# An adaLN block on one core: where norm 1's scale and shift are applied, the split of row transpositions, and the order at the entry of mixing

## The chip, the cores and the metric

The kernel runs on one core of a Trainium2 chip. Its time is the device time in microseconds; the median of the kernel before over three runs is 1981.68 us (1977.05 to 1985.39). The engines are TensorE (PE, with its weight loads shown apart as PEld), VectorE (DVE), ScalarE (ACT), GpSimd (POOL) and SyncE (SP), which issues most transfers. PE writes its results to PSUM, which has eight banks; each PSUM tile here takes one.

## The reference

One sequence of S = 2048 rows, D = 576 columns, F = 4608, 32 heads of 18 columns, a causal window of 256. `w_mod` makes six vectors from a condition vector `c`; the first two shift and scale the first layer norm.

```python
mod = (_silu(c) @ w_mod).reshape(c.shape[0], 6, 1, -1)
sa, ca, ga, sb, cb, gb = (mod[:, 0], mod[:, 1], mod[:, 2], mod[:, 3], mod[:, 4], mod[:, 5])
h = _layernorm(x) * (1 + ca) + sa
x = x + ga * _A_ref(h, A_wqkv, A_wo)      # attention: qkv, softmax over 256 keys, @ wo
h = _layernorm(x) * (1 + cb) + sb
x = x + gb * _B_ref(h, B_w1, B_w2, B_w3, B_w4)

# _B_ref(x, w1, w2, w3, w4)
h = _gelu(_layernorm(x) @ w1)             # mixing: the four quarters of h's columns
hs = shifted(h) @ w2                      # are shifted by +1, -1, +2, -2 rows
x1 = x + hs
return x1 + _gelu(_layernorm(x1) @ w3) @ w4   # channel MLP
```

All inputs and the output are f32.

## The kernel before

**Products.** Each large matmul is made of three products of a high and a low part of both operands (fp32r), over four chunks of 128 of D and a tail of 64: 14 instructions per output tile (`products`). So every weight and every activation is split: a copy to fp32r gives the high part, a subtraction the low part. A chunk of the tail holds high and low part above each other in one 128-row chunk.

**Order.** The program is a list of events (time, function) that `play` runs in the order of their times. In the attention phase PE's instructions keep this order, while the other engines' are placed by the framework's scheduler, as PE's are in the later phases. The unit of time in attention is one attention unit: 4 heads and 512 queries, 32 of them (4 query groups, `g`, by 8). Times below zero are the prologue. A function that asks for a tile of a tag waits, on the chip, until an earlier tile of that tag is free: the number of buffers of each tag (`self.pb` for PSUM) therefore sets who waits for whom.

**Prologue.** `cond` computes SiLU of `c`. `mod_col` (L218) computes one vector of the modulation with 25 narrow products per vector (one column each), all in f32: the scale `ca` first, the shift `sa` later. The scale goes into the weights: `w_split` multiplies each chunk of Wqkv by `ca` (ACT for the high part, DVE for the low part, L242, five of each per chunk), `v_split` does so for the V weights (L270). The shift becomes a bias: `w_bias` (L250, per chunk of 128 columns of Q and K) and `v_bias` (L281), added when the projections are evicted.

**Rows to columns.** `x_norm` normalizes a block of 128 rows (on DVE, L108, or ACT, L106), `x_tr` transposes it with `split9`: the main part (L69, four transpositions into one bank, then the ACT copy L70 and the DVE subtraction L71) and the tail (L73, then L74 and L75). In the prologue main and tail have two banks, afterwards both take the one bank of tag "tr". The result `hT` holds 512 rows.

**Attention.** Projections of Q and K (L311, 14 instructions, one bank of tag "mm") are evicted by ACT (L333) and DVE (L334) into the tile `qe` and go to DRAM; those of V are evicted by DVE (L364). From DRAM Q and K come back per unit. Scores (L393) go through banks of tag "sc" to a masked maximum on DVE (L394), 16 score tiles per unit; their transposed counterpart X (L427) goes through "st" to the exponential on ACT (L440); `av` (L451) and its transposition (L463, into the tile of tag "oT") end a unit, and the rows go to DRAM. The PSUM banks are:

```python
self.pb = {"sc": 3, "st": 2, "av": 1, "mm": 1, "tr": 1}
```

The projections of group g+1 and the modulation's vectors 2 to 5 (`modvec`, POOL, L483) are spread between the units of group g.

**Output projection.** `s4(t)` reads 128 attention rows (`or` or `s4rows`) from DRAM, transposes them with `split9` into the single tile of tag "oT", multiplies by Wo (L616), adds the residual, normalizes twice and writes rows `xn` for mixing. Row blocks 0 to 11 run beside the last units of attention; blocks 12 to 15 at the start of mixing, with event times from -0.7 on, while the times of mixing itself count from 0.

**Mixing and MLP.** `stage1` loads normalized rows and transposes them (`xnT`), `stage2` multiplies by w1 (L771) and applies the GELU and the shifts, `stage3` multiplies by w2 (L822), normalizes and transposes again (`LT`). The channel MLP goes over 18 groups of 256 of F: up (L896), GELU (L902), down (L921), accumulation (L925); its weights are loaded and split by `weights(fg)` (L88 and L89), for the first group at the start of the phase.

Of the kernel before, what the change touches and what calls it, by code (L numbers as in the profile page):

```python
# [9 lines left out]
F32 = mybir.dt.float32  # L10
# [8 lines left out]
D = 576  # L19
F = 4608  # L20
P = 128
# [30 lines left out]
class Kern:  # L52
# [12 lines left out]
    def split9(self, row, L, cs, name, tags=("tr", "tr")):  # L65
        nc = self.nc
        pa = self.ps.tile([P, KC, P], F32, tag=tags[0], name=name + "pa", bufs=self.pb[tags[0]])
        for k in range(KC):
            nc.tensor.transpose(pa[:, k, :], row[:, k * P:(k + 1) * P], self.ident)  # L69
        nc.scalar.copy(L[:, 0:KC, cs], pa)  # L70
        nc.vector.tensor_tensor(out=L[:, KC:2 * KC, cs], in0=pa, in1=L[:, 0:KC, cs].bitcast(F32), op=ALU.subtract)  # L71
        pb = self.ps.tile([TAIL, P], F32, tag=tags[1], name=name + "pb", bufs=self.pb[tags[1]])
        nc.tensor.transpose(pb, row[:, KC * P:D], self.ident)  # L73
        nc.scalar.copy(L[:TAIL, 2 * KC, cs], pb)  # L74
        nc.vector.tensor_tensor(out=L[TAIL:, 2 * KC, cs], in0=pb, in1=L[:TAIL, 2 * KC, cs].bitcast(F32), op=ALU.subtract)  # L75
# [37 lines left out]
    def setup(self, stack):  # L113
# [11 lines left out]
        self.identb = self.cst.tile([P, P], BF16, name="identb")  # L125
        nc.vector.tensor_copy(self.identb, self.ident)
# [9 lines left out]
    def phase_a(self):  # L136
# [9 lines left out]
        self.pb = {"sc": 3, "st": 2, "av": 1, "mm": 1, "tr": 1}  # L146
        with ExitStack() as st:
# [7 lines left out]
            maskb = kp.tile([P, 2, P], BF16, name="maskb")  # L155
            silu = kp.tile([P, KC + 1], F32, name="silu")
            sa = kp.tile([P, KC + 1], F32, name="sa")
            ca = kp.tile([P, KC + 1], F32, name="ca")
            bqk = kp.tile([P, 9], F32, name="bqk")
            bv = kp.tile([P, D], F32, name="bv")  # L160
            ones = kp.tile([P, 1], F32, name="ones")
            pw = None

            def consts():
                nc.gpsimd.memset(ones, 1.0)
                for i in range(3):
                    nc.gpsimd.memset(Q[i].bitcast(F32), 0.0)
                    nc.gpsimd.memset(K[i][96:128].bitcast(F32), 1.0)
                    if i == 0:
                        nc.gpsimd.memset(mask, 0.0)  # L170
                        nc.gpsimd.affine_select(out=mask[:, 0:P], in_=mask[:, 0:P], pattern=[[1, P]], compare_op=ALU.is_gt, fill=NEG, base=0, channel_multiplier=-1)
                        nc.gpsimd.affine_select(out=mask[:, 2 * P:], in_=mask[:, 2 * P:], pattern=[[-1, P]], compare_op=ALU.is_ge, fill=NEG, base=0, channel_multiplier=1)
                        nc.gpsimd.memset(maskb, 0.0)
                        nc.gpsimd.affine_select(out=maskb[:, 1, :], in_=maskb[:, 1, :], pattern=[[1, P]], compare_op=ALU.is_ge, fill=NEG, base=0, channel_multiplier=-1)
                        nc.gpsimd.affine_select(out=maskb[:, 0, :], in_=maskb[:, 0, :], pattern=[[-1, P]], compare_op=ALU.is_gt, fill=NEG, base=0, channel_multiplier=1)
                        for v in V[:4]:
                            nc.gpsimd.memset(v, 1.0)
                for v in V[4:]:
                    nc.gpsimd.memset(v, 1.0)
# [3 lines left out]
            def cond():  # L183
                ct = sm.tile([P, KC + 1], F32, name="ct", bufs=1)
                nc.vector.memset(ct, 0.0)
                with nc.allow_non_contiguous_dma("condition vector to partitions"):
                    nc.sync.dma_start(ct[:, 0:KC], self.c[0, 0:KC * P].rearrange("(k p) -> p k", p=P))
                    nc.sync.dma_start(ct[:TAIL, KC:KC + 1], self.c[0, KC * P:].rearrange("(k p) -> p k", p=TAIL))
# [788 lines left out]
```

## Time and profile before

| | |
|---|---|
| median of three runs | 1981.68 us (1977.05 to 1985.39) |
| profiled execution, own time | 1975.25 us |
| its span | 1973.5 us |
| PE busy | 1819.9 us, 92% |
| DVE busy | 961.7 us, 49% |
| ACT busy | 634.0 us, 32% |
| POOL busy | 384.4 us, 19% |
| HBM read, written | 107.81 MB, 50.73 MB |

The stages by their spans: the first score starts at 104.27 us; projections are interleaved with attention until about 629; then the output projection takes their place until 852.8; mixing begins and ends between there and about 1041; the channel MLP runs from 1070 to the end. A profile row of a group gives its line, engine, operation, output and inputs with their shape, the count, and behind the bar the busy time, the mean time of one in ns, and the idle time of the engine just before them with what ended most of it. A timeline row gives the start, the length and in brackets how long the engine had been idle and what released it. Rows of waits give, for a line, whom its engine stood idle for, the idle time in us and how often.

### The profile page before, as it was taken

What the parts mean: (1) busy time and instruction counts of PE and PEld (TensorE: products, weight loads), DVE (VectorE), ACT (ScalarE), POOL (GpSimd) and SP (SyncE); (2) the same over time, 40 slices, a digit from 0 to 9 for tenths busy, and PEclk for the clock granted to TensorE, in tenths of its full rate; (3) what the DMA queues carried; (4) which work ended last, traced back from release to release, by engine and by line L of the source; (5) the groups of instructions that cost most, each with busy time, mean ns of one, the idle gap of its engine ahead of it and who ended that gap; (6) DMA issues with size and microseconds to landing.
All of it is one profiled execution on the core that took longest, in us unless ns stands there. A gap on an engine that the chain in (4) does not pass through costs nothing.

```text
span 1973.5 us, 30348 instructions
## 1 busy us (share of the span) xinstructions
PE 1819.9 (92%) x11690; PEld 1546.0 (78%) x11690; DVE 961.7 (49%) x2604; ACT 634.0 (32%) x1177; POOL 384.4 (19%) x410
## 2 busy tenths in 40 slices
PE   6888897998999878869998999999999999999999
PEld 5765675776676666657897999999999999999998
DVE  4355465555566656545675344333433344334433
ACT  2214344444445444424322222222222222222211
POOL 5000012010000212210015332333332112111100
PEclk6797999998999898989999999999999999999999
DMA  5332344343445444243322111111111000000002
GB/s 162 114 108 90 102 146 119 109 143 90 118 125 164 134 138 135 81 141 103 116 97 81 50 43 32 50 50 50 50 51 39 26 26 25 21 21 18 1 1 96
DMA packets 128776, 161.20 MB, mean 82 GB/s; under 512 B 35124, under 2 KB 69940, under 8 KB 128632
## 3 DMA queue, kind: packets, MB, share of 16 engines
q1 hardware_dynamic: 113880, 136.32, 23.3%
q10 hardware_dynamic: 14752, 22.94, 3.4%
q8 instruction: 92, 1.51, 0.3%
q14 instruction: 52, 0.43, 0.1%
HBM read 107.81 MB, written 50.73 MB: 80 GB/s over the span
## 4 chain that ended last, share of the span: by engine, by line
PE 81%; DVE 7%; POOL 4%; DMA 3%; ACT 3%; issue 2%; SPq 1%; ACTq 0%; POOLq 0%; DVEq 0%
PE p L921 23%; PE p L896 23%; PE qk L311 6%; PE X L427 4%; PE sc L393 4%; PE av L451 4%; PE v L311 3%; PE pg L771 3%; PE po L616 2%; PE X L436 2%; PE w L822 2%; DVE sc L394 1%; DVE qe L334 1%; DMA wr<-in_A_wqkv_dram 1%; POOL s4rows L627 1%
## 5 line engine op out<-in xcount | busy, mean ns | idle before, releaser
L921 PE MATMUL p<-W,Gc 128*128 128x288 f32 x3456 | 481.8, 295 | 7.7 <-ACT W L88 4.6
L921 PEld LDWEIGHTS p<-W,Gc 128*128 128x128 f32 x3456 | 473.2, 188 | 19.7 <-ACT W L88 5.1
L896 PE MATMUL p<-LNT,W 128*128 128x512 f32 x2016 | 484.1, 391 | 0.1
L896 PEld LDWEIGHTS p<-LNT,W 128*128 128x128 f32 x2016 | 371.9, 188 | 69.9 <-DVE W L89 0.8
L394 DVE CUSTOM_DVE_ANT_0 sc<-sc,mask 128x384 f32<-128x384 f32 (+2 forms) x512 | 271.3, 542 | 183.5 <-PE sc L393 181.3
L440 ACT ACTIVATE P<-X 128x512 f32<-128x512 f32 (+2 forms) x384 | 215.7, 570 | 294.2 <-PE X L436 239.1
L925 DVE TENSOR_TENSOR accA<-p,accA 128x288 f32<-128x288 f32 x340 | 151.9, 454 | 317.6 <-PE p L921 315.7
L900 ACT ACTIVATE gfc<-p 128x512 f32<-128x512 f32 x144 | 86.0, 597 | 659.3 <-PE p L896 659.3
L393 PE MATMUL sc<-K,Q 108*128 108x384 f32 (+2 forms) x512 | 199.6, 396 | 7.9 <-DVE m L394 4.8
L925 DVE TENSOR_TENSOR accB<-p,accB 128x288 f32<-128x288 f32 x204 | 92.5, 456 | 198.1 <-PE p L921 196.3
L311 PE MATMUL qk<-hT,Wc 128*128 128x512 f32 x504 | 166.8, 432 | 14.4 <-DVE qe L334 13.7
L427 PE MATMUL X<-Q,K 110*128 110x128 f32 (+2 forms) x704 | 170.0, 317 | 7.2 <-ACT P L440 7.0
L427 PEld LDWEIGHTS X<-Q,K 110*128 110x128 f32 x704 | 130.0, 199 | 45.2 <-ACT P L440 20.0
L89 POOL TENSOR_TENSOR W<-r,W 128x576 fp32r<-128x576 f32 x34 | 49.1, 1444 | 451.6 <-ACT W L88 451.6
L436 PE MATMUL X<-maskb,identb 128*128 128x256 bf16 (+1 forms) x640 | 124.5, 261 | 0.0
L393 PEld LDWEIGHTS sc<-K,Q 108*128 108x128 f32 x512 | 102.0, 202 | 28.6 <-issue 9.8
L903 DVE TENSOR_TENSOR Gc<-gfc,Gc 128x512 fp32r<-128x512 f32 x144 | 118.5, 823 | 11.3 <-ACT Gc L902 7.6
L311 PEld LDWEIGHTS qk<-hT,Wc 128*128 128x128 f32 x504 | 89.9, 201 | 30.3 <-DVE qe L334 15.5
L451 PE MATMUL av<-P,V 128*32 128x384 f32 (+2 forms) x1408 | 106.1, 415 | 0.0
L311 PE MATMUL v<-Wv,hT 128*128 128x288 f32 x448 | 85.8, 314 | 10.6 <-DVE qe L334 9.4
L902 ACT CAST Gc<-gfc 128x512 fp32r<-128x512 f32 x144 | 89.3, 620 | 3.6
L311 PEld LDWEIGHTS v<-Wv,hT 128*128 128x128 f32 x448 | 68.0, 194 | 16.8 <-DVE qe L334 12.7
(1092 smaller groups left out, 1773.9 us busy)
## 6 DMA issues: line engine op xcount, KB each, us to landing
K<-k0d SPq DMA_DIRECT2D x96, 108.0 KB
r<-in_B_w_dram SPq DMA_DIRECT2D x36, 288.0 KB
Q<-q0d SPq DMA_DIRECT2D x128, 72.0 KB
wm<-in_w_mod_dram SPq DMA_DIRECT2D x24, 288.0 KB
K<-k1d SPq DMA_DIRECT2D x48, 108.0 KB
x<-in_A_x_dram SPq DMA_DIRECT2D x16, 288.0 KB
Q<-q1d SPq DMA_DIRECT2D x64, 72.0 KB
od<-o SPq DMA_DIRECT2D x32, 144.0 KB
```

Source lines behind the costliest of these rows:

```text
L311: nc.tensor.matmul(pm, pl()[i][0], pl()[i][1], start=(i == 0), stop=(i == 13))
L393: nc.tensor.matmul(sc[:, lo:], q[0:2 * R3, h, i * P:(i + 1) * P], k[0:2 * R3, h // 2, i * P + lo:(i + 3) * P], start=True, stop=True)
L394: nc.vector.tensor_tensor_reduce(out=sc[:, lo:], in0=sc[:, lo:], in1=mask[:, lo:], scale=1.0, scalar=-3e38, op0=ALU.add, op1=ALU.max, accu ...
L427: nc.tensor.matmul(x[:, p0 * P:(p0 + w) * P], k[0:2 * R3 + 2, h // 2, (kb + 2) * P:(kb + 3) * P], q[0:2 * R3 + 2, h, q0 * P:(q0 + w) * P], ...
L436: nc.tensor.matmul(x[:, p0 * P:(p0 + w) * P], self.identb, m, start=False, stop=(n == len(ms) - 1))
L440: nc.scalar.activation(pt[:, c0:c1, h % 2, :], x[:, c0 * P:c1 * P].rearrange("p (a b) -> p a b", b=P), AF.Exp, scale=SCALE)
L451: nc.tensor.matmul(abox[0][32 * h:32 * h + 32, q0 * P:(q0 + w) * P], v[:, hh * VA:hh * VA + 32], Pt[b, h // 2][:, p0:p0 + w, h % 2, :], st ...
L896: nc.tensor.matmul(pg, w, a, start=(i == 0), stop=(i == len(pl) - 1))
L902: nc.scalar.copy(Gh, gf)
L903: nc.vector.tensor_tensor(out=Gl, in0=gf, in1=Gh.bitcast(F32), op=ALU.subtract)
L921: nc.tensor.matmul(po, a, w, start=(i == 0), stop=(i == len(seq) - 1))
L925: nc.vector.tensor_tensor(out=acc[t][:, cs], in0=po, in1=acc[t][:, cs], op=ALU.add)
```

## The change

**Prologue.** The condition vector is loaded from ACT's queue, and the exponential's table is loaded before it arrives. Both modulation vectors come in five transfers ahead of the rows. `mod_sum` replaces `mod_col`: the shift is summed on PE by ten wide products (256 and 320 columns) with SiLU spread over 128 columns, the scale by multiply-adds on DVE whose 128 partial sums `mod_cols` adds up with two products with ones. Ten DVE multiply-reduces with the identity turn both rows into columns. Weights are split without a scale (two ACT copies and two subtractions per chunk), and `w_bias` and `v_bias` are gone.

**Scale and shift.** `x_tr(g, k)` transposes chunk k of four row blocks into one bank; ACT evicts it with scale and bias into a tile `h` (one buffer; in the prologue the two buffers of `qe`), POOL casts it to the high part, DVE subtracts. The evictions of projections lose their bias; V's moves from DVE to ACT.

**Banks and order.** Scores have two banks, projections two. `split9` gives main and tail as two functions, which s4 places 0.12 of a unit apart and mixing 0.005. The last four blocks of s4 move behind the start of mixing, between its first products; `weights(0)` moves into mixing, and the vector `gb` is loaded at mixing's start. The setting of constants is in two parts, and the second is later.

```diff
-        self.pb = {"sc": 3, "st": 2, "av": 1, "mm": 1, "tr": 1}
+        self.pb = {"sc": 2, "st": 2, "av": 1, "mm": 2, "tr": 1}
...
+            def mod_sum(k):
+                def f():
+                    kk = P if k < KC else TAIL
+                    w = wm["t"][:kk, k, :]
+                    for i, (c0, c1) in enumerate(half):
+                        if k == 0:
+                            wm[0, i] = ps([P, 512], "sc", f"pms{i}")
+                        nc.tensor.matmul(wm[0, i][:, 0:c1 - c0], wm["s"][:kk, k, :], w[:, c0:c1], start=(k == 0), stop=(k == KC))
+                    a = wm["a"][:kk]
+                    if k == 0:
+                        nc.vector.tensor_scalar(a, w[:, D:], silu[:kk, k:k + 1], None, op0=ALU.mult)
+                    else:
+                        nc.vector.scalar_tensor_tensor(out=a, in0=w[:, D:], scalar=silu[:kk, k:k + 1], in1=a, op0=ALU.mult, op1=ALU.add)
+                return f
+
+            def mod_cols():
+                for i, (c0, c1) in enumerate(half):
+                    wm[1, i] = ps([P, 512], "st", f"pmc{i}")
+                    nc.tensor.matmul(wm[1, i][:, 0:c1 - c0], ones.to_broadcast([P, P]), wm["a"][:, c0:c1], start=True, stop=True)
+                for v, dst in ((0, sa), (1, ca)):
                     for j in range(KC + 1):
...
+                        nc.vector.tensor_tensor_reduce(out=pm, in0=pm, in1=self.ident[:n, :n], scale=1.0, scalar=float(v), op0=ALU.mult, op1=ALU.add, accum_out=dst[:n, j:j + 1])
...
-                    for k in range(KC + 1):
-                        h, l = (k, KC + k) if k < KC else (2 * KC, 2 * KC + 1)
-                        nc.scalar.activation(w[:, h, :], raws[c][:, k, :], AF.Copy, scale=ca[:, k:k + 1])
-                        nc.vector.scalar_tensor_tensor(out=w[:, l, :], in0=raws[c][:, k, :], scalar=ca[:, k:k + 1], in1=w[:, h, :].bitcast(F32), op0=ALU.mult, op1=ALU.subtract)
+                    self.split(w[:, 0:KC, :], w[:, KC:2 * KC, :], r[:, 0:KC, :], nc.scalar.copy, nc.vector.tensor_tensor)
+                    self.split(w[:, 2 * KC, :], w[:, 2 * KC + 1, :], r[:, KC, :], nc.scalar.copy, nc.vector.tensor_tensor)
...
+            def x_tr(g, k):
...
+                    pa = ps([P, 4, P], "tr" if g else ("tr", "mm", "mm", "av", "tr")[k], f"hT{g}_{k}")
+                    for i in range(4):
+                        nc.tensor.transpose(pa[:n, i, :], xrows[4 * g + i][:, k * P:k * P + n], self.ident)
+                    if g:
+                        h = kp.tile([P, 512], F32, tag="h32", name=f"h{g}_{k}", bufs=1)
+                    else:
+                        h = kp.tile([P, 2, 512], F32, tag="qe", name=f"h{g}_{k}", bufs=2)[:, 0, :]
+                    nc.scalar.activation(h[:n], pa[:n].rearrange("p a b -> p (a b)"), AF.Identity, bias=sa[:n, k:k + 1], scale=ca[:n, k:k + 1])
...
+                    nc.gpsimd.tensor_copy(hi, h[:n])
+                    nc.vector.tensor_tensor(out=lo, in0=h[:n], in1=hi.bitcast(F32), op=ALU.subtract)
...
-                    tt = w0 - 0.75 + 0.18 * i
-                    ev += [(tt - 1.2, x_load(4 * g + i)), (tt - 0.6, x_norm(4 * g + i)), (tt, x_tr(4 * g + i))]
+                    tt = w0 - 0.8
+                    ev += [(tt - 1.2 + 0.1 * i, x_load(4 * g + i)), (tt - 0.6 + 0.1 * i, x_norm(4 * g + i))]
+                ev += [(w0 - 0.8 + 0.16 * k, x_tr(g, k)) for k in range(KC + 1)]
...
-        return list(zip(self.d4, (load, tr, wo(0), wo(1), ln1, ln2)))
-    d4 = (-0.6, 0.0, 0.3, 0.55, 0.8, 1.3)
+        return list(zip(self.d4, (load, begin, trb, wo(0), wo(1), ln1, ln2)))
+    d4 = (-0.6, 0.0, 0.12, 0.3, 0.55, 0.8, 1.3)
...
-        ev = [(-1.5, begin), (-0.9, w2t)]
+        ev = [(-1.5, begin), (-0.9, w2t), (3.05, lambda: self.weights(0))]
         for i in range(4):
-            ev += [(-0.7 + 0.15 * i + 0.15 * d, f) for d, f in self.s4(12 + i)]
+            ev += [(0.12 + 0.12 * i + 0.12 * d, f) for d, f in self.s4(12 + i)]
```

Three places show how PE's order moves. PE in the prologue, before, behind the warm-up products: `pmc` are the narrow products of the modulation, `hT0pa` and `hT0pb` main and tail of a row block's transposition, `pb` the bias of a weight chunk, `qk` a projection.

```order
L218 MATMUL pmc_278<-silu,wm 128x1 x20
L218 MATMUL pmc_278<-silu,wm 64x1 x5
L69 MATMUL hT0pa<-ident,x_228 128x128 x4
L73 MATMUL hT0pb<-ident,x_228 64x128
L69 MATMUL hT1pa<-ident,x_230 128x128 x4
L73 MATMUL hT1pb<-ident,x_230 64x128
L69 MATMUL hT2pa<-ident,x_232 128x128 x4
L73 MATMUL hT2pb<-ident,x_232 64x128
L69 MATMUL hT3pa<-ident,x_234 128x128 x4
L73 MATMUL hT3pb<-ident,x_234 64x128
L218 MATMUL pmc_403<-silu,wm 128x1 x20
L218 MATMUL pmc_403<-silu,wm 64x1 x5
```

The same place after, from the last products of the shift: `pms` are the wide products of the modulation, `pmc` now the sums over the partial sums, and `hT_0` and `hT_1` the first two chunks of four row blocks.

```order
L226 MATMUL pms_262<-wm,silub 128x256
L226 MATMUL pms_264<-wm,silub 128x320
L237 MATMUL pmc_319<-acc_193,ones 128x256
L237 MATMUL pmc_321<-acc_193,ones 128x320
L304 MATMUL hT_0_338<-ident,x_234 128x128
L304 MATMUL hT_0_338<-ident,x_236 128x128
L304 MATMUL hT_0_338<-ident,x_238 128x128
L304 MATMUL hT_0_338<-ident,x_240 128x128
L304 MATMUL hT_1_347<-ident,x_234 128x128
L304 MATMUL hT_1_347<-ident,x_236 128x128
L304 MATMUL hT_1_347<-ident,x_238 128x128
L304 MATMUL hT_1_347<-ident,x_240 128x128
```

The narrow products and the biases are gone from the row, and a group of transpositions now fills one bank from four row blocks instead of one bank from one block.

PE beside the output projection, before, at the fifth row block (`oTT4pa` main, `oTT4pb` tail; `sc27` scores of unit 27, `X25` the transposed scores of unit 25):

```order
L393 MATMUL sc27_0_1_7289<-K0_170,Q0_167 128x384
L408 MATMUL mT26_7292<-identr_73,mr26_7259 8x128 x4
L393 MATMUL sc27_0_2_7309<-K0_170,Q0_167 128x384
L69 MATMUL oTT4pa_7313<-ident_68,s4rows_6298 128x128 x4
L73 MATMUL oTT4pb_7320<-ident_68,s4rows_6298 64x128
L427 MATMUL X25_2_1_7324<-Q1_168,K1_171 128x256 x2
L436 LDWEIGHTS identb_75
```

The same block after, from the main part to the tail:

```order
L71 MATMUL oTT4pa_7154<-ident_68,s4rows_6139 128x128 x4
L436 MATMUL X25_2_1_7161<-Q1_166,K1_169 128x256 x2
L445 LDWEIGHTS identb_173
L445 MATMUL X25_2_1_7161<-maskb_172,identb_173 128x256
L402 MATMUL sc27_0_3_7166<-K0_168,Q0_165 128x384
L460 MATMUL av25_7064<-P25_1_0_7037,V3_158 32x384 x2
L460 MATMUL av25_7064<-P25_1_2_7078,V3_158 32x384 x2
L460 MATMUL av25_7064<-P25_1_0_7037,V0_155 32x128 x2
L460 MATMUL av25_7064<-P25_1_2_7078,V0_155 32x128 x2
L436 MATMUL X25_2_2_7190<-Q1_166,K1_169 128x256 x2
L445 LDWEIGHTS identb_173
L445 MATMUL X25_2_2_7190<-maskb_172,identb_173 128x256
```

Two rows further on, after one more score, stands the tail `oTT4pb`; before, it stood right behind the main part.

PE at the start of mixing, before: `oT31` is the last attention step, `oTT12` to `oTT14` and `po` the last blocks of the output projection, `xnT0` the first normalized rows of mixing.

```order
L463 MATMUL oT31_8960<-ident_68,avs31_8958 128x128 x4
L69 MATMUL oTT12pa_9024<-ident_68,or12_9019 128x128 x4
L73 MATMUL oTT12pb_9031<-ident_68,or12_9019 64x128
L616 MATMUL po12_0_9037<-Wo_6204,oT12_9023 128x288 x14
L69 MATMUL oTT13pa_9089<-ident_68,or13_9053 128x128 x4
L73 MATMUL oTT13pb_9096<-ident_68,or13_9053 64x128
L616 MATMUL po12_1_9059<-Wo_6204,oT12_9023 128x288 x14
L616 MATMUL po13_0_9113<-Wo_6204,oT13_9088 128x288 x14
L69 MATMUL xnT0pa_9153<-ident_68,xn0_9035 128x128 x4
```

The same place after; `pg0` are mixing's first products (w1):

```order
L472 MATMUL oT31_8801<-ident_68,avs31_8799 128x128 x4
L71 MATMUL xnT0pa_8871<-ident_68,xn0_8862 128x128 x4
L77 MATMUL xnT0pb_8878<-ident_68,xn0_8862 64x128
L71 MATMUL xnT1pa_8882<-ident_68,xn1_8864 128x128 x4
L77 MATMUL xnT1pb_8889<-ident_68,xn1_8864 64x128
L71 MATMUL xnT2pa_8893<-ident_68,xn2_8866 128x128 x4
L77 MATMUL xnT2pb_8900<-ident_68,xn2_8866 64x128
L71 MATMUL xnT3pa_8904<-ident_68,xn3_8868 128x128 x4
L77 MATMUL xnT3pb_8911<-ident_68,xn3_8868 64x128
L786 MATMUL pg0_4_8938<-xnT0_8870,W14_6465 128x512 x2
L786 MATMUL pg0_0_8990<-xnT0_8870,W10_6636 128x512 x2
L71 MATMUL xnT4pa_8928<-ident_68,xn4_8915 128x128 x4
```

Four row blocks of mixing and its first products now come ahead of `oTT12`, which stands four rows below the last of these.

## The prediction before the run

> **What bounds the kernel now.** I read the first page for the busy shares and the granted TensorE clock, then cut the span into stages at points of the program, then looked in each stage at what ended PE's waits.
>
> ```profile
> span 1973.5 us, 30348 instructions
> PE 1819.9 (92%) x11690; PEld 1546.0 (78%) x11690; DVE 961.7 (49%) x2604; ACT 634.0 (32%) x1177; POOL 384.4 (19%) x410
> PEclk6797999998999898989999999999999999999999
> ```
>
> ```profile
> 0.00:104.27 104.27, 78.18 (x347) 64.07 (x347) 38.46 (x103) 26.52 (x68) 29.98 (x48) 0.71 0.45 133
> 104.27:629.00 524.73, 470.01 (x3391) 353.53 (x3391) 307.36 (x1025) 221.10 (x405) 44.51 (x56) 0.95 0.40 117
> 629.00:852.80 223.80, 184.72 (x1464) 141.24 (x1463) 125.70 (x432) 101.86 (x178) 52.86 (x72) 0.92 0.42 127
> 852.80:925.00 72.20, 52.21 (x274) 44.29 (x274) 39.33 (x98) 26.17 (x50) 6.68 (x16) 0.86 0.47 152
> 1041.00:1070.00 29.00, 20.86 (x94) 16.38 (x92) 13.73 (x21) 10.42 (x23) 21.42 (x18) 0.88 0.34 105
> 1070.00:1973.50 903.50, 899.84 (x5392) 821.85 (x5390) 357.55 (x713) 210.20 (x376) 217.24 (x171) 1.00 0.12 36
> ```
>
> The columns are stage, length, busy time of PE, PEld, DVE, ACT and POOL, PE's granted clock, DMA share and GB/s. PE is the bound everywhere, but only the channel MLP after 1070 is full (899.84 of 903.50 at clock 1.00), and the change hardly touches it. Before 1070 PE is idle for 26.1 us (start, A), 54.7 (attention with projections, B), 39.1 (attention with output projection, C), 20.0 (entry of mixing, D) and 8.1 (entry of the MLP, F). It also loses to the clock, which alternates between full and half: time at half is 2 × (1 − clock) × length, 52 us in B, 36 in C, 20 in D, 7 in F. Half of that times PE's busy share is lost: about 23, 15, 7 and 2.5 us. So the change is worth what it takes of these waits and of the clock behind them.
>
> **A, the start.**
>
> ```profile
> 10.71 10.05 PE L218 MATMUL pmc<-silu,wm 128*128 128x1 f32 x50 [2.69 <-DVE silu L192]
> 21.22 0.46 DVE L96 BATCH_NORM_STATS2 a0st<-x 128x6 f32<-128x288 f32 x1
> 24.98 6.12 DVE L242 SCALAR_TENSOR_TENSOR Wc<-wr,ca,Wc 128x128 fp32r<-128x128 f32 x15
> 31.15 0.57 DVE L108 TENSOR_SCALAR x<-x,a1mv,a1rs 128x576 f32<-128x576 f32 x1
> 32.12 1.11 PE L69 MATMUL hT0pa<-ident,x 128*128 128x128 f32 x4 [11.35 <-ACT x L106]
> 33.31 0.56 ACT L70 CAST hT<-hT0pa 128x512 fp32r<-128x512 f32 x1
> 33.91 0.69 DVE L71 TENSOR_TENSOR hT<-hT0pa,hT 128x512 fp32r<-128x512 f32 x1
> 40.81 10.38 PE L218 MATMUL pmc<-silu,wm 128*128 128x1 f32 x50
> 59.53 3.46 PE L311 MATMUL qk<-hT,Wc 128*128 128x512 f32 x8
> 66.06 1.26 PE L250 MATMUL pb<-sa,wr 128*128 128x1 f32 x10
> 74.23 5.60 PE L281 MATMUL pbv<-wvr,sab 128*128 128x288 f32 x20
> 104.27 0.73 PE L311 MATMUL qk<-hT,Wc 128*128 128x512 f32 x2
> 105.10 0.30 DVE L394 CUSTOM_DVE_ANT_0 sc<-sc,mask 128x128 f32<-128x128 f32 x1 [0.56 <-PE sc L393]
> ```
>
> ```profile
> GB/s 0 186 152 347 315 364 373 314 390 358 242 290 358 279 249 2 0 0 0 0 0 0 5 286 165 151 97 226 71 0 5 94 0 0 0 0 0 0 0 0
> L270 DVE SCALAR_TENSOR_TENSOR Wv<-wvr,ca,Wv 128x576 fp32r<-128x576 f32 x5 | 3.9, 817 | 0.0
> L483 POOL TENSOR_SCALAR wm<-wm,silu 128x576 f32<-128x576 f32 (+1 forms) x20 | 15.0, 755 | 218.5 <-DMA wm<-in_w_mod_dram 218.5
>   DVE qe L334: 4.7, 3
>   DVE V L364: 1.7, 3
> ```
>
> The first of these rows is the transfer rate in 40 slices of the first 60 us, the last two are the waits of the projections, L311, between 50 and 104.27: time that PE stood idle, times, and for whom. Now the scale costs 10.05 us of narrow products, the weight splits need it (DVE, 6.12 us), the row norms stand behind the splits, then 32.12 to 40.81 goes into transpositions and 10.38 us into the shift; the first projection ends at 59.53 + 3.46 = 63.0 and the first score's neighbour starts at 104.27.
>
> After: SiLU is ready at 10.7 as now and spread over 128 columns by 11.5. The two vectors' weights, 576 × 1152 × 4 bytes = 2.65 MB, now come ahead of the rows of x; the first seven slices above moved (0 + 186 + 152 + 347 + 315 + 364 + 373) × 1.5 us = 2.6 MB, so they land by about 11 and cost nothing. Scale on DVE: five steps like L270, 5 × 0.82 = 4.1, to 15.6. Shift on PE: ten wide products, nearest the 20 of L281 (0.28 each, twice that at half rate), 5.6, to 17.1; two more for the scale, 18.2. DVE then has 8 statistics (0.46), 10 column extractions with the identity (0.30, and I add half again for the read-back: 0.45), two norms (0.57), a weight split (0.7) and small steps (about 1.5): 3.7 + 4.5 + 1.1 + 0.7 + 1.5 = 11.5, so the transpositions start at 27. Each of five pieces passes ACT (0.56), POOL (nearest L483, 755 × 512/576 = 0.67; at worst twice that, when two operands are read) and DVE (0.69) through two buffers: three rounds of 2.2 us with hand-overs, plus about 3 us of splits queued between, to 37. The first projection ends at 38, 25 us earlier. Of the 41.3 us from there to 104.27 go the V bias (5.6), five bias groups (1.3 each, 6.5) and the bank waits (6.4), while the clock comes back later relative to the work (about 3 us more): 25.8. First score at 63.8: **−41 us**, between −28 (extraction and POOL at twice the price, 13 us) and −48. The Q and K rows still go through DRAM; about 16 us of V and K projections cover that, and each us beyond costs one.
>
> **B and C, attention.**
>
> ```profile
>   DVE oT L71: 26.2, 12
>   DVE hT L71: 21.9, 12
>   DVE qe L334: 18.4, 18
> PE sc L393 <- DVE m L394: 4.8, 4, 2.1
> ```
>
> The first two are why the tail transposition (L73) waited, the third is L311 from 104.27 to 629. In B the transposition of rows waits 21.9 us for DVE's subtraction, since the tail needs the one bank; in the changed order a bank is freed by ACT alone, and the next piece comes 0.16 of an attention unit later (32 units end at 852.8, so one is about 748 / 32 = 23.4 us and 0.16 of it 3.7 us), so −21.9. Two banks take −16 of 18.4. Two bias groups go: −2.5. Added: about 2 us for the single 512-wide buffer of the eviction, about 3 us because in the second block POOL's second cast stands behind a modulation chunk that waits for a DMA (DVE and the scores queue behind that cast), and the scores' third bank. In C the tail comes 0.12 of a unit, 2.8 us, after the main part: of 26.2 I leave 4, for DVE's late answers.
>
> ```profile
> 109.21 0.43 DVE L394 CUSTOM_DVE_ANT_0 sc<-sc,mask 128x256 f32<-128x256 f32 x1 [0.62 <-PE sc L393]
> 109.48 0.40 PE L393 MATMUL sc<-K,Q 108*128 108x256 f32 x2
> 821.94 0.60 DVE L394 CUSTOM_DVE_ANT_0 sc<-sc,mask 128x384 f32<-128x384 f32 x1
> 822.13 0.44 PE L393 MATMUL sc<-K,Q 108*128 108x384 f32 x1 [1.02 <-DVE m L394]
> ```
>
> With two banks a score waits for the maximum two scores earlier. I compared every score's start with that: 43 of 512 began before it ended (these are the first pair, 109.60 against 109.64, and the last, 822.13 against 822.54), by 25 us in sum, 7 in B and 17.5 in C; the other 469 lose nothing. The end below is 0, since PE's present stalls also hold back the DVE work in that queue; I take the 25. The V eviction moves from DVE to ACT, busy 221.10 of 524.73: hidden, unless an exponential falls behind it.
>
> Clock: the waits that go are where it drops; of 23 and 15 I count 14 and 8. B: −21.9 − 16 − 2.5 + 2 + 3 + 7 − 14 = **−42** (−15 to −70). C: −22 + 17.5 − 8 = **−13** (+10 to −30).
>
> **D and F.**
>
> ```profile
> PE oTT12pa L69 <- DMA or<-od: 11.4, 1, 11.4
> PE p L921 <- ACT W L88: 4.6, 1, 4.6
> PE p L921 <- ACT Gc L902: 1.9, 1, 1.9
> ```
>
> D: now PE waits 11.4 us for the last attention rows from DRAM. In the changed order four row blocks are transposed and the first mixing products run meanwhile. They can start only when the last attention output has left the tile they share; I put that at 4 us. Then a row block takes 8.7 / 4 = 2.2 us (32.12 to 40.81) where the main part keeps PE for 1.1: four of them, 4 to 5 us idle. Later hand-overs I put at 4. That is 13 against 20.0; with the clock **−10** (0 to −16). F: the first MLP weights are split before mixing ends; 7 of 8.1 us idle and 2 of clock: **−9** (−3 to −11). Main and tail 0.005 apart in mixing keep PE's order: nothing.
>
> Sum: −41 − 42 − 13 − 10 − 9 = −115; 1973.5 − 115 = 1858.5 us of span. The profiled execution itself took 1975.25 us, 1.75 more than its span, and the median of the runs, 1981.68, is 1.0033 of that: (1858.5 + 1.75) × 1.0033 = **1866 us**.
>
> **Rivals.** (1) *Scores' banks:* DVE's queue is denser once PE no longer stalls, and two banks cost twice my 25 us, and C's clock stays (8): 1866 + 33 = 1899. For: DVE is busy 59% in B. Against: 469 of 512 have slack. (2) *The eviction chain:* ACT, POOL, DVE through one buffer takes longer than 4 us, PE waits about 2 us at each of 15 pieces, and B's 5 us of clock there is not won: 1866 + 35 = 1901. For: POOL's queue holds modulation chunks (218.5 us of DMA waits). Against: DVE and POOL need 1.4 us of the 4.
>
> (3) *The clock does not come back.*
>
> ```profile
> 470.00:480.00 10.00, 8.60 (x46) 5.97 (x45) 5.46 (x15) 3.47 (x7) 1.42 (x2) 0.50 0.29 77
> PE hT13pb L73 <- DVE hT L71: 1.4, 1, 1.4
> ```
>
> Between 470 and 480 the clock was 0.50 with no wait over 1.4 us. If it drops for another cause than these waits, the 22 us of B and C stay: 1888. [...]
>
> (4) *Slower: DVE becomes the bound.* If maxima and subtractions fill DVE so that every score waits for its bank, a mean wait of x costs 512 × x; from x = 0.25 us (126 us) the result is over 1991. At 0.32: 1866 + 164 = 2030. Against: it needs nearly every score to wait, where the count found one in twelve, and DVE loses the V evictions.
>
> **Chances.** Forecast 0.62, (1) 0.13, (2) 0.09, (3) 0.08, (4) 0.08. About 0.5% (10 us) is what can be told from no change. Forecast and (1) to (3) are all faster, 0.92; I move 0.02 to "same" for several of them together. The range takes the lower ends of A to F part of the way (1812) and the upper ends with the first three rivals (1940: (1) and (2) together are 1934), and leaves out (4).
>
> **What would show it.** First score near 64 us; no waits of tail transpositions on DVE; L311 waits of a few us; score waits on DVE of 20 to 30 us, mostly beside the output projection; clock of at least 0.97 in B; mixing's first product about 15 us after the last attention step; no stretch of idle PE at the MLP's entry. It is wrong if the first score is later than 80, if the score waits pass 60 us, or if PE waits for the evicted pieces in B.

## The result and the profile after

The changed kernel takes 1884.64 us (median of four runs, 1882.53 to 1890.93) against 1981.35 us (median of four runs taken beside it): a ratio of 0.9518, 95% interval 0.9487 to 0.9548. The forecast was 1866 us, so the change brought 97 us of the 115 that the stages were to give.

The first page of the changed kernel's profile (this execution took 1890.93 us):

```profile
span 1888.8 us, 29893 instructions
PE 1774.5 (94%) x11504; PEld 1505.6 (80%) x11504; DVE 939.0 (50%) x2543; ACT 635.6 (34%) x1169; POOL 396.1 (21%) x430
PEclk7979999999999989899999999999999999999999
```

Both kernels cut at the same points of the program: first score, first transposition of the output projection, last attention step, first up product, end (before, the first cut is at the projection beside the first score, 0.5 us ahead of it). The stages are named A to D and F as in the prediction, but D is now all of mixing, and F runs from the first up product to the end. Columns as in the prediction. Before, then after:

```profile
0.00:104.27 104.27, 78.18 (x347) 64.07 (x347) 38.46 (x103) 26.52 (x68) 29.98 (x48) 0.71 0.45 133
104.27:632.10 527.83, 473.11 (x3411) 354.95 (x3410) 308.98 (x1030) 222.48 (x407) 44.51 (x56) 0.95 0.40 118
632.10:852.50 220.40, 181.32 (x1445) 139.74 (x1442) 124.06 (x425) 100.49 (x175) 52.62 (x72) 0.92 0.41 124
852.50:1041.40 188.90, 167.02 (x1018) 149.44 (x1017) 119.16 (x314) 63.84 (x129) 18.66 (x47) 0.95 0.36 116
1041.40:1973.50 932.10, 920.30 (x5480) 837.83 (x5477) 371.00 (x733) 220.62 (x398) 238.65 (x188) 1.00 0.13 38
```

```profile
0.00:64.20 64.20, 44.27 (x182) 31.95 (x183) 30.73 (x79) 19.57 (x38) 24.18 (x44) 0.81 0.60 176
64.20:568.20 504.00, 464.72 (x3390) 349.06 (x3388) 293.29 (x993) 231.84 (x430) 62.97 (x80) 0.96 0.44 128
568.20:784.20 216.00, 181.85 (x1441) 140.12 (x1442) 124.74 (x425) 99.77 (x176) 52.69 (x72) 0.94 0.41 127
784.20:961.00 176.80, 164.59 (x1017) 146.59 (x1016) 123.09 (x318) 68.06 (x139) 29.49 (x55) 0.97 0.42 132
961.00:1888.80 927.80, 919.12 (x5480) 837.90 (x5478) 367.16 (x729) 216.35 (x389) 226.76 (x181) 1.00 0.13 37
```

The stages gave, in this order: A 40.1 us, B 23.8, C 4.4, mixing (D) 12.1 and the entry of the MLP with what follows (F) 4.3, in sum 84.7. That is 12 less than the medians say, because the profiled execution of before took 1975.25 us, 6 under its median, and that of after is the longest of its four. Part of it sits in B: five kernels below run the same instructions up to the end of B, and B took 498.4 to 503.7 us in them, 504.0 here. B is therefore worth 24 to 29 us against the one profile of before.

What PE waited for afterwards: waits of the scores for the maxima in B, then in C; and, out of the lists of two lines, the tail transposition's (L77) on the subtraction and the projections' (L321):

```profile
PE sc L402 <- DVE m L403: 15.8, 14, 4.3
PE sc L402 <- DVE m L403: 9.4, 7, 2.0
  DVE oT L73: 8.2, 5
  DVE hT L313: 2.3, 2
```

The 18.4 us of projection waits and the 21.9 us of waits between main and tail in B are gone. In C the tail still waits 8.2 us. The score waits grew from 4.8 to 25.1 us, in 21 places. In B the row transpositions (L304, before L69) also wait longer, 8.3 us against 3.6, mostly for steps of attention.

### The profile page after: what moved, and what is told of

Same layout as the page of the kernel before. It is cut to its first block, busy times and chain, and to the rows that moved or that the text cites. A ratio compares the mean times of both kernels' runs of the same rounds, so it can differ in the third digit from the quotient of the medians.

```text
span 1888.8 us, 29893 instructions
## 1 busy us (share of the span) xinstructions
PE 1774.5 (94%) x11504; PEld 1505.6 (80%) x11504; DVE 939.0 (50%) x2543; ACT 635.6 (34%) x1169; POOL 396.1 (21%) x430
## 4 chain that ended last, share of the span: by engine, by line
PE 80%; DVE 6%; DMA 5%; POOL 5%; issue 2%; ACT 2%; ACTq 0%; SPq 0%; POOLq 0%; DVEq 0%
PE p L911 24%; PE p L936 24%; PE qk L321 5%; PE sc L402 4%; PE X L436 4%; PE av L460 3%; PE pg L786 3%; PE po L627 2%; PE v L321 2%; PE X L445 2%; PE w L837 2%; DVE sc L403 1%; DMA wm<-in_w_mod_dram 1%; POOL s4rows L638 1%; POOL s4rows L639 1%
## 5 line engine op out<-in xcount | busy, mean ns | idle before, releaser
L402 PE MATMUL sc<-K,Q 108*128 108x384 f32 (+2 forms) x512 | 203.2, 399 | 33.7 <-DVE m L403 25.1
L321 PE MATMUL qk<-hT,Wc 128*128 128x512 f32 x504 | 163.4, 425 | 2.3 <-DVE hT L313 2.3
L321 PEld LDWEIGHTS qk<-hT,Wc 128*128 128x128 f32 x504 | 88.8, 198 | 16.4 <-issue 4.8
L321 PE MATMUL v<-Wv,hT 128*128 128x288 f32 x448 | 81.6, 305 | 0.5 <-ACT V L373 0.5
L627 PE MATMUL po<-Wo,oT 128*128 128x288 f32 x448 | 72.0, 312 | 2.1 <-DVE oT L79 1.5
```

What stands on the lines that cost most here:

```text
L321: nc.tensor.matmul(pm, pl()[i][0], pl()[i][1], start=(i == 0), stop=(i == 13))
L402: nc.tensor.matmul(sc[:, lo:], q[0:2 * R3, h, i * P:(i + 1) * P], k[0:2 * R3, h // 2, i * P + lo:(i + 3) * P], start=True, stop=True)
L627: nc.tensor.matmul(po, l, r, start=(n == 0), stop=(n == len(pl) - 1))
```

## The experiments

Each kernel is the changed kernel with the edit shown, unless another is named; its ratio is to the kernel before.

**Banks as before.**

```diff
-        self.pb = {"sc": 2, "st": 2, "av": 1, "mm": 2, "tr": 1}
+        self.pb = {"sc": 3, "st": 2, "av": 1, "mm": 1, "tr": 1}
```

> The changed kernel (1884.6 us) with the PSUM banks of before: three for scores, one for projections. Theory A (the banks are a trade, and nearly even): the scores' waits for DVE's maxima, 25.1 us, fall to about the 8 us of before, and the waits of projections for their eviction come back at about 18 us; the prologue loses 1 to 3 us, since its transpositions use both projection banks. 1884 to 1892. Theory B (the price of two score banks is what is missing in the attention phase): without it the kernel is faster by 15 us or more, 1870. Theory C (two projection banks carry the gain of that stage): slower by 15 us or more, 1900, most of it in projection waits and a lower clock before the first output projection.

1901.56 us, 0.9619 (0.9584 to 0.9655): 17 us slower than the change. Its windows from start to first score, B and C, and the projections' wait:

```profile
0.00:71.30 71.30, 46.10 (x183) 31.37 (x184) 30.28 (x78) 19.81 (x39) 26.24 (x45) 0.86 0.58 171
71.30:590.20 518.90, 465.18 (x3390) 350.99 (x3388) 293.23 (x994) 231.74 (x430) 62.30 (x79) 0.96 0.43 124
590.20:797.00 206.80, 175.96 (x1445) 136.42 (x1442) 123.35 (x425) 99.28 (x175) 52.76 (x72) 0.96 0.43 130
  DVE qe L94: 23.3, 18
```

Theory C holds where projections run: the start is 7 us longer, B 15. Its lower clock doesn't show, though (0.96 in both): the 15 us in B are idle time of PE. And C, which has none of the Q, K and V projections, is 9 us shorter with three score banks (206.8 against 216.0). The trade is good in one stage and bad in the next.

**Tails behind the main part.**

```diff
-    d4 = (-0.6, 0.0, 0.12, 0.3, 0.55, 0.8, 1.3)
+    d4 = (-0.6, 0.0, 0.0, 0.3, 0.55, 0.8, 1.3)
```

> The changed kernel with the tail of each output-projection transposition directly behind its main part, as before. Theory A (by its own waits): tail waits rise from 10.7 us to about 26 us and the clock beside them falls a little: 15 us of waits and 2 to 5 us of clock, 1900 to 1905. Theory B (the waits only move: PE waits at the scores' two banks instead, since DVE has the same work): score waits fall as the tail waits rise, and the time is within 6 us of 1884.6.

1898.66 us, 0.9607 (0.9568 to 0.9645), 14 us slower. C and the tail's wait:

```profile
561.00:791.20 230.20, 191.49 (x1446) 145.62 (x1442) 125.89 (x425) 101.01 (x175) 52.71 (x72) 0.89 0.40 119
  DVE oT L73: 23.0, 12
```

Theory A has the size, not the split. C is 14.2 us longer, but PE's idle time there rises by only 4.6 us (230.20 - 191.49 against 216.00 - 181.85); the other 9.6 us are longer busy time, 191.49 against 181.85, at a clock of 0.89 instead of 0.94. The tail waits themselves rose by 12.3 us, from 10.7 to 23.0, so most of that was made up for by shorter waits of other steps, as theory B says of the waits.

**The last output rows ahead of mixing.**

```diff
-            ev += [(0.12 + 0.12 * i + 0.12 * d, f) for d, f in self.s4(12 + i)]
+            ev += [(-0.7 + 0.15 * i + 0.15 * d, f) for d, f in self.s4(12 + i)]
```

> The changed kernel with the last four blocks of the output projection placed ahead of mixing, as before. Theory A: the wait for the last attention rows from DRAM (11.4 us before) comes back and with it the 12 us by which the stretch from the last attention step to the last product of mixing became shorter: 1895 to 1898. Theory B (the old order would do as well in the changed kernel, because the tail now has other places and loads come earlier): within 5 us of 1884.6.

1902.63 us, 0.9616 (0.9582 to 0.9651). The stretch D and its longest wait:

```profile
775.20:966.90 191.70, 167.24 (x1019) 148.72 (x1017) 123.41 (x318) 68.49 (x139) 29.26 (x55) 0.96 0.39 122
PE oTT12pa L71 <- DMA or<-od: 11.6, 1, 11.6
```

Theory A: the wait for the rows is back, and D is 14.9 us longer than after the change.

**The MLP's first weights, three ways.** First their event alone, then the load of `gb` too, then also the tile of `gb` in the pool that reuses mixing's memory.

```diff
-        ev = [(-1.5, begin), (-0.9, w2t), (3.05, lambda: self.weights(0))]
+        ev = [(-1.5, begin), (-0.9, w2t)]
...
-        ev = []
+        ev = [(-0.5, lambda: self.weights(0))]
```

> The changed kernel with the first MLP weights loaded and split at the start of the MLP phase, as before. Theory A (prediction's: the early place takes away 8 to 9 us of waits and clock): 1893. Theory B (the early place has put five multiplications into POOL's queue ahead of a row norm's small steps, so that PE waits 5.1 us for the last transposition of mixing in place of 7.7 us for the weights): the old place costs 3 to 5 us, 1888 to 1890, the 5.1 us wait of the last row block is gone, and the waits of the first down products (4.6 and 1.9 us before) are back.

```diff
-            nc.sync.dma_start(self.gb, self.modd[5].to_broadcast([P, D]))
...
         gb = self.gb
+        nc.sync.dma_start(gb, self.modd[5].to_broadcast([P, D]))
```

> The changed kernel with both the first MLP weights and the load of the vector gb at the start of the MLP phase, as before. The run with the weights alone put back had the same order of POOL and the same 5.1 us wait of the last row block as the changed kernel, at 1887.6 us. Theory A (it is gb's early load that lets POOL multiply and split MLP weights ahead of the last row norm): the 5.1 us wait is gone, the waits for the weights behind the first up products are back (7.7 us before), and the stretch from the first up product to the end is 3 to 6 us longer: 1888 to 1891. Theory B (neither place matters): 1883 to 1887, with the 5.1 us wait still there.

```diff
-            self.gb = self.bc.tile([P, D], F32, name="gb")
-            nc.sync.dma_start(self.gb, self.modd[5].to_broadcast([P, D]))
...
-        gb = self.gb
+        self.gb = gb = cp.tile([P, D], F32, name="gb")
+        nc.sync.dma_start(gb, self.modd[5].to_broadcast([P, D]))
```

> The changed kernel with the first MLP weights at the start of the MLP phase and the tile of gb allocated there too, in the memory that the mixing phase has left, as before (putting back only the place in the program left the order of POOL as it was, 1887 us). Theory A (the tile's memory holds gb's load back until mixing is over, and that kept POOL free for the last row norm): the 5.1 us wait of the last row block is gone, waits of 5 to 8 us of the first down products for the weights are back, and from the first up product to the end the kernel takes 2 to 6 us longer than the changed kernel's 927.8: 1886 to 1891. Theory B (something else of the change brought the wait): the wait is still there, 1884 to 1888.

1887.64 us (0.9545), 1887.09 (0.9530) and 1889.37 (0.9544, 0.9519 to 0.9568); none can be told from the change by its time. In the first two the 5.1 us wait of the last row block is still there: both theories of the first run fell, and theory B of the second (neither place matters) held. Only the third brings the old waits back, as its theory A says. Its stretch D, the stretch from the first up product to the end, and two waits; then the first products of weights with `gb` on POOL, in the changed kernel and in the third:

```profile
781.20:953.70 172.50, 163.75 (x1019) 146.16 (x1017) 118.09 (x314) 64.20 (x129) 18.94 (x47) 0.97 0.40 127
953.70:1887.30 933.60, 920.62 (x5479) 838.51 (x5477) 371.33 (x733) 220.62 (x398) 238.90 (x188) 1.00 0.13 38
PE p L935 <- ACT W L93: 4.7, 1, 4.7
PE LT15pa L71 <- DVE xm L113: 0.4, 1, 0.4
868.13 1.43 POOL L885 TENSOR_TENSOR r<-r,gb 128x576 f32<-128x576 f32 x1
960.86 4.65 POOL L883 TENSOR_TENSOR r<-r,gb 128x576 f32<-128x576 f32 x3 [5.30 <-DMA gb<-modd]
```

It is the memory of `gb` that decides when POOL may begin with the MLP's weights: SP issues its load at 788.4 in the changed kernel, at 786.9 and 798.9 in the first two, and at 957.2 in the third, where POOL waits 5.3 us for it. Early, the last stretch is 5.8 us shorter (927.8 against 933.6), and mixing 4.3 us longer (176.8 against 172.5): the net is 1.5 us.

**The condition vector on SP.**

```diff
-                    nc.scalar.dma_start(ct[:, 0:KC], ...)
-                    nc.scalar.dma_start(ct[:TAIL, KC:KC + 1], ...)
+                    nc.sync.dma_start(ct[:, 0:KC], ...)
+                    nc.sync.dma_start(ct[:TAIL, KC:KC + 1], ...)
```

> The changed kernel with the condition vector's two small loads issued on SP ahead of the modulation weights, instead of on ACT's queue. In the changed kernel they land at 14.4 us, behind 3.8 MB of weights and rows; before they had landed at 4.9. Theory A (SiLU holds up the whole prologue): PE's wide products start at about 8 us instead of 16.2, as the weights' chunks arrive, and the first score comes 5 to 8 us earlier: 1877 to 1880. Theory B (the row statistics and norms on DVE and POOL, or the weights' transfers, are next in line): under 3 us, 1882 to 1885, with SiLU ready early all the same.

1878.80 us, 0.9494 (0.9465 to 0.9523). The interval overlaps that of the change, so the time alone doesn't settle it; the timeline does. PE, first products of the modulation, and the end of them:

```profile
7.80 3.07 PE L226 MATMUL pms<-wm,silub 128*128 128x256 f32 x12
14.37 1.24 PE L237 MATMUL pmc<-acc,ones 128*128 128x256 f32 x4
```

The products start at 7.80 instead of 16.21, and the first score comes at 55.3, against 62.1 to 64.2 in the profiles of six kernels that share this prologue. Theory A, but the size is not firm: in the last kernel below, with the same edit, the products start at 11.57 and the first score comes at 60.6. The edit has a second effect that this run doesn't part from the first: SP issues the load of the first weight chunk at 7.89 instead of 14.40.

**More warm-up products.**

```diff
-            ev += [... (-9.04, warm(24)), ...]
+            ev += [... (-9.04, warm(62)), ...]
```

> The changed kernel with 62 instead of 24 warm-up products in the prologue, so that PE is busy until about 16 us, when SiLU is ready. Theory A (the clock goes to half when PE was busy less than about half of a stretch of 3.4 us): the clock is full when the modulation's products start, and they take 4 to 5 us instead of 7.75; the half-clock stretch from 10.9 to 21.1 us is gone. [...] The time itself: 0 to 3 us less.

1885.28 us, one run. PE in the prologue:

```profile
16.96 5.21 PE L226 MATMUL pms<-wm,silub 128*128 128x256 f32 x20
23.13:26.54 3.41, 0.53 (x2) 0.14 (x1) 1.68 (x6) 1.55 (x4) 3.27 (x5) 1.00 0.89 282
```

The products take 5.21 us instead of 7.75, of which, in the changed kernel, the first 4.98 us ran at a clock of 0.50. The second row is the stretch ahead of the next half clock, which lasts from 26.54 to 40.19: it holds 0.53 us of work, but also the start of a wait of 3.95 us, so this run doesn't show whether the little work or the one long wait counts. The first score is no earlier (66.7), since the transpositions behind the products wait for row norms. The clock of this stretch was not what held the prologue.

**Transpositions in the projections' banks.** All transpositions of the attention phase use the tag "mm" (in the prologue two of the five chunks of rows take a score bank); their own bank goes to the scores, or to the shared banks. A third kernel is the one before with a score bank given to its transpositions.

```diff
-                        pt = ps([P, 4, 4, 32], "tr", f"oT{u}")
+                        pt = ps([P, 4, 4, 32], "mm", f"oT{u}")      # and so for the other transpositions
...
-        self.pb = {"sc": 2, "st": 2, "av": 1, "mm": 2, "tr": 1}
+        self.pb = {"sc": 3, "st": 2, "av": 1, "mm": 2}      # first
+        self.pb = {"sc": 2, "st": 2, "av": 1, "mm": 3}      # second
...
-        self.pb = {"sc": 3, "st": 2, "av": 1, "mm": 1, "tr": 1}
+        self.pb = {"sc": 2, "st": 2, "av": 1, "mm": 1, "tr": 2}      # kernel before
```

> The changed kernel with three banks for scores and two shared by projections and all transpositions of the attention phase (the bank of the transpositions goes to the scores). Theory A (scores need the third bank only beside the output projection, projections need the second one before): score waits fall from 25 us to about 8, projection waits stay under 8 us, tail waits stay near 11: 10 to 18 us less, 1867 to 1875. Theory B (transpositions now wait for the projections' banks, since a projection holds one for a whole accumulation): their waits take back the gain or more: 1885 to 1900.

> The kernel with transpositions in the projections' banks, but with two banks for scores and three shared ones, instead of three and two (that one: 1856.3 us, of which the stretch beside the output projection took 190.6 us against 216.0 in the changed kernel). Theory A (it was the scores' third bank): score waits back at 25 to 33 us, 1875 to 1885. Theory B (it was the second bank that a tail transposition can take while the main part still stands in the first; tail waits were 1.4 us there against 10.7): the stretch beside the output projection stays under 198 us and the time is 1852 to 1862.

> The kernel before (1979.3 us) with one change: a bank of the scores goes to the transpositions (two each). Theory A (main and tail of a transposition no longer wait for each other, so the 21.9 and 26.2 us of tail waits go, and half or more of the clock beside them comes back; the scores lose about 20 us as they did in the changed kernel): 1930 to 1950. Theory B (the waits move to the scores, whose maxima stand in the same DVE queue): 1965 to 1985.

1856.30 us (0.9382, 0.9356 to 0.9409), 1864.13 (0.9420, 0.9393 to 0.9446) and 1944.61 (0.9839, 0.9803 to 0.9876). C in the three, then the score waits on the maxima over the whole first and second kernel:

```profile
559.30:749.90 190.60, 173.47 (x1445) 135.74 (x1442) 121.65 (x425) 97.60 (x175) 52.77 (x72) 0.97 0.47 142
558.20:759.00 200.80, 178.90 (x1445) 138.14 (x1442) 123.31 (x425) 98.27 (x175) 52.81 (x72) 0.96 0.45 134
611.60:812.40 200.80, 178.68 (x1445) 138.18 (x1442) 123.76 (x425) 98.18 (x175) 52.72 (x72) 0.96 0.44 135
  DVE m L404: 13.1, 11
  DVE m L404: 25.5, 25
```

With a second bank that transpositions can take, C falls from 216.0 to 200.8 us, also in the old kernel, where it was 220.4; the third score bank takes another 10. The waits of tails for the subtraction are 1.4 us in the first kernel's C and none in the other two. So the tail's time in the order was the lesser remedy for its wait: a second bank does more. The first kernel is faster than either of its theories said, because neither had the tail's second bank. In the second, the time lies just outside theory B's range, and the stretch is 2.8 us over theory B's 198, because the score waits came back as theory A says: both hold, the tail's bank for the larger part. The old kernel came out as theory A had it.

**Together.** The first of these, the condition vector on SP, and the second group's MLP weights split on DVE:

```diff
-        l = (nc.vector if fg == 0 else nc.gpsimd).tensor_tensor
+        l = (nc.vector if fg <= 1 else nc.gpsimd).tensor_tensor
```

> The three findings together: transpositions in the projections' two banks with three for scores (28 us less by itself), the condition vector's loads on SP ahead of the weights (6 us less), and the second group's MLP weights split on DVE instead of POOL (POOL then is free for the last row norm: the 5.1 us wait of the last transposition of mixing should shrink to about 1 us, 4 us less). If they add: 1884.6 - 28 - 6 - 4 = 1847. If the prologue's gain is lost in the attention phase or DVE's extra splits delay mixing's end: 1852 to 1858.

1853.53 us, 0.9365 (0.9338 to 0.9393), the shortest here, 31 us under the change, though not to be told from 1856.30. The three do not add, as the second of the two cases had it. The last row block still waits, now for DVE, where the new splits stand ahead of its norm (PE, then DVE):

```profile
932.81 1.09 PE L71 MATMUL LT15pa<-ident,xm 128*128 128x128 f32 x4 [4.17 <-DVE xm L113]
926.21 1.31 DVE L94 TENSOR_TENSOR W<-W_1r,W 128x128 fp32r<-128x128 f32 x1
```

## Why the prediction was right, and where it was not

The time lies inside the range, and every stage moved the way that was forecast, but the sizes of B, C and F were too large. Of the signs named ahead, the first score (64.2 us), the projection waits (2.3), the score waits in sum (25.1) and the first mixing product (12 us after the last attention step) came. Four others didn't: tails of C still wait for DVE (8.2 us), more of the score waits lie in B than beside the output projection (15.8 and 9.4), B's clock was 0.96, and PE is idle for 5.1 us at the MLP's entry.

**A: 41 forecast, 40.1 measured, by two errors that cancel.** PE and, in the third row, ACT in the changed prologue:

```profile
16.21 7.75 PE L226 MATMUL pms<-wm,silub 128*128 128x256 f32 x20 [8.35 <-DVE silub L201]
37.87 2.49 PE L321 MATMUL qk<-hT,Wc 128*128 128x512 f32 x8
14.47 0.21 ACT L196 ACTIVATE silu<-ct 128x5 f32<-128x5 f32 x1 [12.25 <-DMA x<-in_A_x_dram]
43.85 8.69 PE L321 MATMUL qk<-hT,Wc 128*128 128x512 f32 x30 [1.87 <-DVE hT L313]
```

The step "SiLU is ready at 10.7 as now" failed: its input landed about 14.4, since the load moved to another queue and shared the transfers with all the weights. (The row names a transfer of x; that it was the vector's own load shows in the run with the vector on SP, where this instruction starts at 5.33.) The wide products took 7.75 us instead of 5.6. The first projection ended near 44.5 rather than 38. From there to the first score I allowed 25.8 us, and 19.7 were needed: I added 3 us for a clock that comes back later, and it was higher in this stretch than in that of before, 0.91 against 0.88. That the two errors came out even is luck. The run with the vector on SP puts the cost of the first at 7 to 9 us of its profile and 5.8 us of the median.

**B: 42 forecast, 24 to 29 measured.** The two large removals came out as worked: the 21.9 us of tail waits are gone, and of 18.4 us of projection waits under 3 are left. PE's idle time fell by 15.4 us (54.7 to 39.3), where the steps gave 25.9. The term that failed is the added waits: the scores wait 15.8 us for maxima, where none did before and 7 were counted, and 4.3 of them at the place that the prediction named, in the second block; the row transpositions add 4.7. DVE and PE there, with POOL's chunk ahead:

```profile
131.45 0.74 POOL L492 TENSOR_SCALAR wm<-wm,silu 64x576 f32<-64x576 f32 x1 [2.86 <-DMA wm<-in_w_mod_dram]
134.25 0.69 DVE L313 TENSOR_TENSOR hT<-h,hT 128x512 fp32r<-128x512 f32 x1 [5.28 <-POOL hT L312]
135.39 0.58 PE L402 MATMUL sc<-K,Q 108*128 108x256 f32 x1 [4.33 <-DVE m L403]
```

POOL's cast stands behind a chunk that waits for a DMA, DVE behind the cast, the maxima behind DVE. The 14 us of clock were the other miss: at 0.95 before and 0.96 after, time at half fell only from 53 to 40 us; with the 0.98 of two other kernels with the same instructions in B it would have been 20, so part of this miss is chance of the execution.

**C: 13 forecast, 4.4 measured.** Four terms were off. The tails kept more waits than the 4 left over: 10.7 us in all. The two score banks cost 4.6 us (9.4 less the 4.8 of before), not 17.5: over both stages the count gave 25 us and 20.4 came (15.8 + 4.6), but the places were exchanged, since the count moved no start of any other instruction. The 8 us of clock did not come: 0.92 to 0.94, with the busy time the same (181.32 and 181.85). And no term stood for the other steps: PE's idle time in C beside tails and scores grew from 8.1 to 14.0 us, mostly waits for DVE and for the exponential.

**D: 10 forecast, 12.1 measured, and 14.9 when undone.** The mixing's first product started 12 us after the last attention step; about 15 were named. With the early load of `gb` undone, D took 172.5 us, so the new order is worth 16.4, and 4.3 of them went to pay for F.

**F: 9 forecast, 4.3 in the last stretch, at most 1.5 net.** The step that failed is "the first MLP weights are split before mixing ends": they are, but no term stood for POOL's queue, where splits of the second group's weights now stand ahead of the last row norm. The last stretch is 4.3 us shorter than before (5.8 when undone), and mixing pays 4.3 for it. POOL's subtraction ahead of the norm's small step, DVE behind that, and PE:

```profile
964.55 1.26 POOL L94 TENSOR_TENSOR W<-W_0r,W 128x512 fp32r<-128x512 f32 x1
965.78 0.22 POOL L104 TENSOR_SCALAR d15rs<-d15mv 128x1 f32<-128x1 f32 x1
966.69 0.40 DVE L106 SCALAR_TENSOR_TENSOR d15rs<-d15mv,d15rs 128x1 f32<-128x1 f32 x1 [3.62 <-POOL d15rs L105]
968.89 1.08 PE L71 MATMUL LT15pa<-ident,xm 128*128 128x128 f32 x4 [5.06 <-DVE xm L113]
```

**The rivals.** The score banks (1) cost no more than the 25 us counted. The eviction chain (2) made PE wait only 0.7 us for a piece in B; it did harm at one place, the 4.3 us shown under B. The clock (3) came back in part (B 0.95 to 0.96, C 0.92 to 0.94): it drops for more than single long waits, as the stretch of before that begins at 465.25 shows below, whose longest waits were 1.3 and 1.4 us, with 0.50 after it. DVE did not become the bound (4): 21 of 512 scores waited.

## What to carry to other kernels

A bank that two short steps share in turn was best doubled here: placing the steps apart in time took the tails' wait beside the output projection from 23.0 to 10.7 us, a second bank took it to 1.4 us or none. When a step is moved earlier, its cost is on the queues that it now stands in (here POOL and DVE ahead of a last row norm, with PE idle for 5.1 us), and what holds it back may be the memory of a small tile rather than its place in the program (`gb`: 927.8 against 933.6 us for the last stretch). A tiny load that everything waits for belongs ahead of the large ones: with the condition vector there, the first products started at 7.80 us instead of 16.21.

## What the runs showed of the clock

In the traces of both kernels the granted clock is 1.00 or 0.50, and each period of one value is a whole multiple of 3.41 us long (3.41, 6.83, 10.24 and so on), but for the one that the end of the trace cuts. The changed kernel cut on its grid, then the kernel before on its own:

```profile
447.85:451.27 3.42, 0.71 (x4) 0.27 (x3) 0.62 (x2) 0.73 (x2) 0.00 (x0) 1.00 0.56 80
451.27:454.68 3.41, 3.41 (x13) 2.29 (x17) 0.62 (x2) 0.96 (x2) 0.00 (x0) 0.50 0.62 181
454.68:458.09 3.41, 3.41 (x32) 2.48 (x25) 1.52 (x5) 1.78 (x4) 0.00 (x0) 1.00 0.58 142
```

```profile
465.25:468.66 3.41, 1.60 (x13) 1.12 (x11) 2.15 (x8) 1.42 (x3) 0.00 (x0) 1.00 0.69 238
468.66:472.08 3.42, 2.49 (x18) 0.94 (x18) 1.60 (x4) 0.41 (x2) 0.00 (x0) 0.50 0.52 135
475.49:478.90 3.41, 2.29 (x11) 1.86 (x11) 1.91 (x6) 1.20 (x3) 0.00 (x0) 0.50 0.21 41
478.90:482.32 3.42, 2.05 (x9) 1.55 (x8) 1.65 (x5) 1.76 (x3) 1.40 (x1) 0.50 0.13 51
482.32:485.73 3.41, 3.38 (x22) 1.69 (x23) 0.84 (x3) 0.26 (x1) 0.08 (x1) 0.50 0.28 87
```

One stretch with 0.71 us of work, the rest of it a single wait of 2.7 us, is followed by one at half; that one is full, and the next runs at full clock again. In the kernel before, the stretches with 2.29 and 2.05 us of work are each followed by another at half, though no single wait in the two was longer than 1.4 us. I counted the grid in the traces of all fourteen kernels between 75 and 1050 us. From full clock, a stretch under 45% busy was followed by half in 122 of 122 cases, one of 45 to 65% in 71 of 215, one over 90% in none of 2810. From half, the clock came back after 182 of 197 stretches over 90% and after none of 69 under 65%. This fits the run with the tails behind the main part, where 9.6 of C's 14.2 us were longer busy time, at a clock of 0.89 instead of 0.94. In these traces the drop went mostly with one stretch under about half busy, and the return with a later one that was nearly full; what sets the clock was not shown beyond these counts. With the same instructions in B, six kernels had a clock of 0.96 to 0.98 there and lengths of 498.4 to 504.0 us; I put these microseconds, which no edit explains, down to where the grid falls on the waits, which I have not shown.
